# Output halves in f16 parts from batch 0's third column tile on, in pairs of tiles

## The chip, the cores and the metric

The kernel runs on one NeuronCore of a Trainium2 chip. The metric is the device time of one execution in microseconds (us), smaller is better; it is compared as the median of several runs. The engines are TensorE (PE, matrix products; PEld is its weight load), VectorE (DVE), ScalarE (ACT), GpSimd (POOL) and SyncE (SP), which issues the DMAs.

## The reference

Four batches of 12416 tokens with 128 channels pass two attention steps over 32 induced points, and then a SwiGLU layer with 1536 hidden units:

```
def mab(q, kv):
    s = scale * (q @ kv.transpose(0, 2, 1))
    s = s - s.max(-1, keepdims=True)
    a = np.exp(s)
    a /= a.sum(-1, keepdims=True) + 1e-09
    return a @ kv
h = mab(I, x)                  # (4, 32, 128)
x = mab(x, h)                  # (4, 12416, 128), then reshaped to (49664, 128)
g = x @ w_gate                 # (49664, 1536)
silu = g * (1.0 / (1.0 + np.exp(-g)))
val = x @ w_val
out = silu * val @ w_out       # (49664, 128)
```

All of it is in float32.

## The kernel before

The output of the second attention is never written down: `a @ h @ w` is taken as `a @ (h @ w)`, where h has 32 rows. The attention weights of a column tile (up to 512 tokens) are stacked as high and low parts into 128 rows (`st.stack[c]`), and the products of h with the gate and value weights, also in parts, are the stationary operand (`st.w`, or `st.wn` where the parts are float16).

The work runs in slots. Each batch has 25 column tiles (tile 0 holds 4 blocks of each of four token groups, the other 24 hold 15 or 16 blocks of one group), and each column tile has 12 tiles of 128 hidden units, so 300 slots a batch. A slot has these steps:

- `front`: two matmuls, gate and value, into two PSUM banks
- `gate`: silu on ACT; `value`: the product with the value bank on DVE, giving h
- `split`: a rounded copy (hi, on ACT) and the rest (lo, on POOL, for hidden tiles 1, 5 and 9 on DVE)
- `back`: three matmuls into the output accumulator, `w_lo * hi + w_hi * hi + w_hi * lo`; after the twelfth, `evac` copies the accumulator on DVE and a DMA writes it out

In the first column tile of batch 0 (`u.whole`) h and the output weights are not split, and `back` is one float32 matmul, which the profile shows as two records. In column tiles 1 to 12 of batch 0 the parts are in fp32r (float32 words that PE takes in one pass), with the output weights in `wo_hi` and `wo_lo`. From slot 156 on (`CSW = 13`), and in all later batches, the slots run in pairs (`fronts`, `gates`, `values`, `splits`): the parts are float16, a pair's gate and value lie in two double banks of PSUM, and ACT, DVE and POOL take both slots in one instruction. Sometimes (`u.own`) DVE takes over the split of one of the two. For float16 the values must be scaled by powers of two: `peak_of` and `peak_a` to `peak_d` find the largest weights, `size_a` to `size_u` find the scales from h, `half_a` to `half_c` write the scaled output weights in f16 parts into `keep[2]` and `keep[3]`.

PSUM has 8 banks: two (`ps_o`) for the accumulators and some helpers, six for fronts, as six single banks (`ps_gv`) or as three double ones (`ps_two`). `bank()` hands out one of the six to the other steps.

Each engine works its queue in program order, and the program order is written by hand. `START` and `SECOND` list the start as tokens (`f:3` is the front of slot 3, `g` its silu, `m` its product, `k` its back, `P:0:1` a `peak_of`). `FIRST` and `cur.steps` give the other steps of batch 0 and 1 a slot at which they are put into the queues; `plan` gives the steps of the next batch's attention, and `post` those of a column group's attention weights. In each slot (or pair) the loop puts in the front, the silu, the product, the split of the slot before, the steps due, and then as many backs as keep the number of finished but unused tiles at `ahead`:

```
ahead = min(ahead + (1 if b else size) / RAMP, top_) if nxt is not None and slot < last_burst else max(ahead - 1 / RAMP, low_)
if slot in bursts:
    ahead = low_ - (size == 1)
while len(pend) + sum(len(x.us) for x in wait) > ahead + (slot != slots[-1]):
    back(pend.pop(0))
```

`RAMP` is 6; `top_` and `low_` are 9 and 5 for single slots, 14 and 8 for pairs. Bursts are the slots in which ACT does long exponentials: slot 36 and slot 125 in batch 0 (the second is `nxt.e1`), and one more later. Steps that take an accumulator bank (`acc`) wait until no column tile is about to begin or end.

Of the kernel before, what the change touches and what calls it, by code (L numbers as in the profile page):

```python
# [58 lines left out]
DVE_TILES = {1, 5, 9}  # L59
CAST = {11}  # L60
# [22 lines left out]
al:1:0 g:7 X:o2 pk:5 sh:o2 g:8 low:o2 k:4 pm:5 f:9 jn:o2 pc:5 k:5 f:10 sp:1 m:7 k:6 m:8 f:11 g:9 add:o2 k:7 m:9 g:10 g:11 m:10 m:11 hi:o0 lo:o0 hi:o1  # L83
lo:o1
"""
FIRST = {
    12: "sp:2",
    13: "hi:o2",
    14: "lo:o2",
    15: "sp:3",  # L90
# [11 lines left out]
    54: "m2:70:84",
    56: "sb:56:70:1 m2:84:97",
    59: "sb:70:84:1",
    62: "sb:84:97:1",
# [7 lines left out]
def induced_set_attention_then_swiglu(ctx: ExitStack, tc: tile.TileContext, xt, xn, ind, wgv, wo, out):  # L113
# [120 lines left out]
    joint = {}  # L234

    def half_a(i):
        cs = slice(WP * i, WP * i + WP)
        joint[i] = hp.tile([P, 2 * WF], F32, name="h")[:, :WF]
        nc.gpsimd.tensor_add(out=joint[i], in0=wo_hi[:, cs].bitcast(F32), in1=wo_lo[:, cs].bitcast(F32))
# [583 lines left out]
    with tc.tile_pool(name="xt0", bufs=NCH - NXT) as xt0, tc.tile_pool(name="xn0", bufs=NCH - NXN) as xn0:  # L823
# [18 lines left out]
        def run(token):  # L842
# [17 lines left out]
            at=f["aT"], ah=lambda q, e=0: f["a_hi"](q, (f["same"], nc.scalar.copy)[e]),  # L860
# [35 lines left out]
    def value(u):  # L896
        n = u.n
        if u.whole:
            u.h = hip.tile([P, WB], F32, name="h_hi")[:, :WF]
        else:  # L900
            u.h = u.v if u.t in DVE_TILES else hp.tile([P, 2 * WF], F32, name="h")[:, :WF]
# [2 lines left out]
    def split(u):
        if u.whole:
            return
        n = u.n
        u.hi = hip.tile([P, WB], F32R, name="h_hi")[:, u.at[1]:u.at[1] + WF]
        u.lo = lop.tile([P, WB], F32R, name="h_lo")[:, u.at[2]:u.at[2] + WF]
        (nc.vector.tensor_copy if u.cast_dve else nc.scalar.copy)(out=u.hi[:, :n], in_=u.h[:, :n])  # L910
        eng = nc.vector if u.t in DVE_TILES or u.last else nc.gpsimd
        eng.tensor_sub(out=u.lo[:, :n], in0=u.h[:, :n], in1=u.hi[:, :n].bitcast(F32))  # L912
# [5 lines left out]
    def fronts(st, b, c, t):  # L918
        us = []
        g, v = two(), two()  # L920
        for k in range(2):
# [40 lines left out]
    def back(u):  # L962
# [54 lines left out]
    for b in range(B):  # L1017
        nxt = attention(b + 1, (one, oneb)[(b + 1) % 2]) if b + 1 < B else None
        if nxt is not None:
            nxt.steps = plan(nxt, PA if b == 0 else PB, b + 1)  # L1020
            if b == 0:
# [5 lines left out]
                cur.steps += [(14 + 6 * i, lambda i=i: peak_of(0, i)) for i in range(6)]  # L1027
                cur.steps += [(66 + 6 * i, lambda i=i: peak_of(1, i)) for i in range(3)]
                small = [lambda f=f, k=k: f(k) for k in range(2) for f in (peak_a, peak_m, peak_b)] + [peak_c, peak_d]
                sizes = [cur.f["size_" + k] for k in "abcdu"]  # L1030
                small[2].acc = small[5].acc = sizes[1].acc = (NT - 1, 0, 1)
                cur.steps += list(zip((48, 53, 58, 84, 88, 94, 98, 101), small)) + list(zip((62, 68, 78, 82, 108), sizes)) + [(97, cur.f["proj_rounds"])]
# [116 lines left out]
```

## Time and profile before

| | |
|---|---|
| median of 3 runs | 1396.9 us (1396.57 to 1397.24) |
| the profiled execution, first to last instruction (span) | 1394.8 us |
| that execution's own time beside the span | not recorded; the runs' median is 2.1 us above the span |
| PE busy | 1380.5 us (99%) |
| ACT busy | 1219.3 us (87%) |
| POOL busy | 1211.2 us (87%) |
| DVE busy | 1139.9 us (82%) |
| granted PE clock, mean | 0.999 of full speed |

Busy time is the union of the records of an engine. Matmuls are pipelined: a record is longer than the distance to the next one's start, so a busy PE is not yet a PE at its peak. Batch 0's slot 12 begins near 55 us, its slot 156 near 245 us.

### The profile page before, as it was taken

How to read it: one execution, taken by the hardware profiler on the slowest of the kernel's cores; microseconds unless marked ns; L12 is line 12 of the kernel's file. 1: busy time of each engine (PE TensorE's matmuls, PEld its weight loads, DVE VectorE, ACT ScalarE, POOL GpSimd, SP SyncE). 2: the span in 40 equal slices, each digit the busy share in tenths (PEclk: the TensorE clock that was granted, in tenths of full speed). 3: DMA queues.
4: the chain of work that ended last, by engine and by line, in shares of the span. 5: the costliest groups of instructions: out<-in, count | busy, mean ns of one | idle time of the engine just before them, and what ended most of it. 6: DMA issues, size and time to landing. Idle time of an engine off the chain costs nothing.

```text
span 1394.8 us, 21845 instructions
## 1 busy us (share of the span) xinstructions
PE 1380.5 (99%) x7480; PEld 707.9 (51%) x7480; DVE 1139.9 (82%) x1548; ACT 1219.3 (87%) x1481; POOL 1211.2 (87%) x748
## 2 busy tenths in 40 slices
PE   8999999999999999999999999999999999999998
PEld 6577687544444444444444445444444444444444
DVE  6889878878888767888888877878888888888887
ACT  4988798889998898899999888889999989989987
POOL 1679778899999889988999988989999989989987
PEclk9999999999999999999999999999999999999999
DMA  9224523201122432111003423211001010010000
GB/s 374 80 74 152 168 85 123 101 27 53 32 85 91 177 127 76 60 52 30 30 29 121 157 76 131 103 40 48 28 28 33 31 37 25 31 37 31 28 29 29
DMA packets 52335, 107.03 MB, mean 77 GB/s; under 512 B 13440, under 2 KB 34432, under 8 KB 52224
## 3 DMA queue, kind: packets, MB, share of 16 engines
q1 hardware_dynamic: 52224, 105.64, 22.4%
q8 instruction: 59, 0.97, 0.3%
q14 instruction: 52, 0.43, 0.1%
HBM read 62.87 MB, written 25.43 MB: 63 GB/s over the span
## 4 chain that ended last, share of the span: by engine, by line
PE 91%; ACT 6%; DVE 2%; issue 1%; POOL 0%; DVEq 0%; ACTq 0%; POOLq 0%
PE gw L929 30%; PE o L973 17%; PE o L974 17%; PE o L975 17%; PE gv L889 2%; PE gv L888 2%; ACT silu L939 1%; PE o L454 1%; PE gw L369 1%; PE o L369 1%; PE gv L369 1%; ACT silu L894 1%; ACT s_all L633 1%; ACT h_hi L910 1%; PE gv L361 1%
## 5 line engine op out<-in xcount | busy, mean ns | idle before, releaser
L956 POOL TENSOR_TENSOR h_lo<-h,h_hi 128x960 f16<-128x960 f32 (+2 forms) x522 | 977.5, 1894 | 101.1 <-ACT h_hi L954 94.5
L946 DVE SCALAR_TENSOR_TENSOR h<-gw,sc,silu 128x960 f32<-128x960 f32 (+3 forms) x524 | 599.7, 1145 | 191.4 <-ACT silu L939 177.6
L939 ACT ACTIVATE silu<-gw,sc 128x960 f32<-128x960 f32 (+2 forms) x523 | 566.8, 1085 | 119.3 <-PE gw L929 51.4
L954 ACT CAST h_hi<-h 128x960 f16<-128x960 f32 (+3 forms) x517 | 480.5, 930 | 2.8 <-DVE h L946 2.4
L973 PE MATMUL o<-h_hi,work 128*128 128x480 f16 (+1 forms) x1044 | 388.2, 372 | 0.0
L975 PE MATMUL o<-h_lo,work 128*128 128x480 f16 (+1 forms) x1044 | 388.2, 372 | 0.0
L974 PE MATMUL o<-h_hi,work 128*128 128x480 f16 (+1 forms) x1044 | 388.2, 372 | 0.0
L929 PE MATMUL gw<-stack,tw 128*128 128x512 f16 (+1 forms) x1200 | 300.6, 373 | 0.4 <-ACT silu L939 0.4
L929 PE MATMUL gw<-stack,work 128*128 128x480 f16 (+1 forms) x888 | 221.3, 371 | 1.9 <-ACT silu L939 1.5
L929 PEld LDWEIGHTS <-tw 128*128 128x128 f16 x1200 | 117.2, 98 | 135.1 <-issue 2.8
L912 POOL TENSOR_TENSOR h_lo<-h,h_hi 128x512 fp32r<-128x512 f32 x108 | 139.8, 1318 | 33.5 <-ACT h_hi L910 24.2
L973 PEld LDWEIGHTS <-work 128*128 128x128 f16 x1044 | 102.3, 98 | 117.7 <-issue 3.4
L975 PEld LDWEIGHTS <-work 128*128 128x128 f16 x1044 | 102.1, 98 | 115.5
L974 PEld LDWEIGHTS <-work 128*128 128x128 f16 x1044 | 102.1, 98 | 114.5 <-issue 0.5
L929 PEld LDWEIGHTS <-work 128*128 128x128 f16 x888 | 86.3, 98 | 101.1 <-issue 7.2
L894 ACT ACTIVATE silu<-gv 128x512 f32<-128x512 f32 x156 | 93.8, 603 | 15.2 <-PE gv L888 12.2
L902 DVE TENSOR_TENSOR h<-gv,silu 128x512 f32<-128x512 f32 x108 | 73.2, 682 | 18.2 <-ACT silu L894 10.4
L946 DVE SCALAR_TENSOR_TENSOR o<-gw,sc,silu 128x480 f32<-128x480 f32 (+1 forms) x99 | 72.1, 728 | 0.0
L956 DVE TENSOR_TENSOR h_lo<-o,h_hi 128x480 f16<-128x480 f32 (+1 forms) x99 | 66.3, 670 | 3.4
L888 PE MATMUL gv<-stack,tw 128*128 128x512 f32 x156 | 65.4, 419 | 2.7 <-ACT silu L894 1.2
L983 DVE TENSOR_SCALAR ob<-o,sc 128x480 f32<-128x480 f32 (+1 forms) x87 | 62.9, 723 | 3.9 <-PE o L975 3.9
L910 ACT CAST h_hi<-h 128x512 fp32r<-128x512 f32 x95 | 58.9, 620 | 8.1 <-DVE h L902 7.4
(217 smaller groups left out, 1111.6 us busy)
## 6 DMA issues: line engine op xcount, KB each, us to landing
xt_sb<-xt SPq DMA_DIRECT2D x32, 896.0 KB, 5.2
xn_sb<-xn SPq DMA_DIRECT2D x18, 896.0 KB, 5.3
out<-ob SPq DMA_DIRECT2D x52, 256.0 KB, 2.0
out<-ob SPq DMA_DIRECT2D x48, 240.0 KB, 2.0
xt_sb<-xt SPq DMA_DIRECT2D x4, 832.0 KB, 4.5
stack<-a_hi SPq DMA_DIRECT2D x96, 30.0 KB, 1.8
stack<-a_lo SPq DMA_DIRECT2D x96, 30.0 KB, 1.8
xn_sb<-xn SPq DMA_DIRECT2D x3, 832.0 KB, 5.1
```

What stands on the lines that cost most here:

```text
L888: nc.tensor.matmul(out=u.g[:, :n], lhsT=st.w[:, wcol(0, t)], rhs=rhs, start=True, stop=True)
L894: nc.scalar.activation(out=u.s[:, :u.n], in_=u.g[:, :u.n], func=AF.Silu)
L902: nc.vector.tensor_mul(out=u.h[:, :n], in0=u.v[:, :n], in1=u.s[:, :n])
L912: eng.tensor_sub(out=u.lo[:, :n], in0=u.h[:, :n], in1=u.hi[:, :n].bitcast(F32))
L929: nc.tensor.matmul(out=x[:, 512 * (u.t - t):][:, :u.n], lhsT=st.wn[:, wcol(k, u.t)], rhs=st.stack[c][:, :u.n], start=True, stop=True)
L939: nc.scalar.activation(out=f(u.s), in_=f(u.g), func=AF.Silu, scale=u.st.g)
L946: nc.vector.scalar_tensor_tensor(out=h, in0=f(u.v), scalar=u.st.k, in1=f(u.s), op0=ALU.mult, op1=ALU.mult)
L954: (nc.vector.tensor_copy if h is u.x else one_wide if u.cast_dve else nc.scalar.copy)(out=f(u.hi), in_=h)
L956: (nc.vector if h is u.x else nc.gpsimd).tensor_sub(out=f(u.lo), in0=h, in1=f(u.hi))
L973: nc.tensor.matmul(out=o[:, :n], lhsT=w_lo[:, ws], rhs=u.hi[:, :n], start=(t == 0), stop=False)
L974: nc.tensor.matmul(out=o[:, :n], lhsT=w_hi[:, ws], rhs=u.hi[:, :n], start=False, stop=False)
L975: nc.tensor.matmul(out=o[:, :n], lhsT=w_hi[:, ws], rhs=u.lo[:, :n], start=False, stop=(t == NT - 1))
```

## The change

- Column tile 1 of batch 0 (slots 12 to 23) no longer splits: h stays float32, and `back` uses the unsplit pieces of the output weights (`pieces["o0"]` to `["o2"]`), as in column tile 0. The functions `split`, `hi`, `lo`, `half_a` and the tiles `wo_hi` and `wo_lo` are gone.
- From slot 24 on (`CSO = 2`), not from 156, the slots run in pairs with h and the output weights in f16 parts. For column tiles 2 to 12 the fronts still use the fp32r weights `st.w` and the fp32r stack; the silu has scale 1 and the product the new scale `st.kf`.
- The peaks and sizes move from slots 14 to 108 to the end of `SECOND` and slots 12 to 21; `half_b` and `half_c` move from slots 106 to 154 to slots 24 to 34 and read the unsplit pieces. `peak_b` and `size_m` take their bank from `bank()`, no longer from `ps_o`.
- In `FIRST` the scores of batch 0's blocks 70 to 97 move from slot 50 to 56, with what follows them. Batch 1's first scores come in two visits of four and three chunks, as in later batches, no longer chunk by chunk.

```diff
+CSO = 2
 SECOND = """ ...
-... g:10 g:11 m:10 m:11 hi:o0 lo:o0 hi:o1
-lo:o1
+... g:10 g:11 m:10 m:11 sza P:0:0 P:0:1 P:0:2 P:0:3
 FIRST = {
-    12: "sp:2",
-    13: "hi:o2",
-    14: "lo:o2",
-    15: "sp:3",
+    12: "sp:2 P:0:4",
+    13: "P:0:5",
+    14: "Pa:0 Pm:0 P:1:0",
+    15: "sp:3 Pb:0 P:1:1",
+    16: "P:1:2",
+    17: "szb Pa:1",
+    18: "szc Pm:1",
+    19: "Pb:1",
+    20: "Pc",
+    21: "Pd szu",
...
-    50: "s2:52:56:1 s2:56:70 s2:70:84:1 s2:84:97:1",
+    50: "s2:52:56 s2:56:70:1",
...
+    56: "s2:70:84 s2:84:97:1 sb:56:70:1",
...
     def peak_b(k):
-        ps = ps_o.tile([P, 512], F32, name="o")
+        ps = bank()
...
-        nc.scalar.activation(out=keep[2][:, cs], in_=joint[i], func=AF.Copy, scale=top[:, 2:3])
+        nc.scalar.activation(out=keep[2][:, cs], in_=pieces[f"o{i}"].w, func=AF.Copy, scale=top[:, 2:3])
...
         def size_c():
             grow(st.sc[:, 0:2], powers[:, 0:2], st.sc[:, 6:7])
             grow(st.g, powers[:, 2:3], st.low)
+            if b == 0:
+                grow(st.kf, powers[:, 4:5], st.sc[:, 6:7])
+                grow(st.kf, st.kf, st.sc[:, 6:7])
...
-            if b == 1:
-                add(v1 if q < NXT else last, "s1", q, q not in (0, NXT))
-        if b > 1:
-            add(v1, "s1_visit", 0, 1, 2, 3)
-            add(last, "s1_visit", 4, 5, 6)
+        add(v1, "s1_visit", 0, 1, 2, 3)
+        add(last, "s1_visit", 4, 5, 6)
...
     def fronts(st, b, c, t):
+        wn = st.wn if b or c >= CSW else st.w
...
+        u.gs, u.vs = (st.g, st.k) if wn is not st.w or b else (1.0, st.kf)
...
-            nc.scalar.activation(out=f(u.s), in_=f(u.g), func=AF.Silu, scale=u.st.g)
+            nc.scalar.activation(out=f(u.s), in_=f(u.g), func=AF.Silu, scale=u.gs)
...
-            nc.vector.scalar_tensor_tensor(out=h, in0=f(u.v), scalar=u.st.k, in1=f(u.s), op0=ALU.mult, op1=ALU.mult)
+            nc.vector.scalar_tensor_tensor(out=h, in0=f(u.v), scalar=u.vs, in1=f(u.s), op0=ALU.mult, op1=ALU.mult)
...
-            w_hi, w_lo = keep[2:4] if u.half else (wo_hi, wo_lo)
+            w_hi, w_lo = keep[2:4]
...
-                cur.steps += [(106 + 6 * i, lambda i=i: (half_a, half_b, half_c)[i % 3](i // 3)) for i in range(9)]
+                cur.steps += [(24 + 2 * i, lambda i=i: (half_b, half_c)[i % 2](i // 2)) for i in range(6)]
...
-            turn = b == 0 and slot2 == NT * CSW
+            turn = b == 0 and slot2 == NT * CSO
```

## Rows read from the trace of the kernel before

**Rows 1.** The page: the span, and PE's busy time.
```profile
span 1394.8 us, 21845 instructions
...
PE 1380.5 (99%) x7480; PEld 707.9 (51%) x7480; DVE 1139.9 (82%) x1548; ACT 1219.3 (87%) x1481; POOL 1211.2 (87%) x748
```
**Rows 2.** Groups by line of PE, 61.4 to 245.5: count, busy us, mean ns, idle.
```profile
L889 PE MATMUL gv<-stack,tw 128*128 128x512 f32 x140 | 56.3, 402 | 1.5 <-ACT silu L894 1.4
L888 PE MATMUL gv<-stack,tw 128*128 128x512 f32 x139 | 54.6, 393 | 1.2 <-ACT silu L894 1.2
L973 PE MATMUL o<-h_hi,wo_lo 128*128 128x512 f32 x136 | 54.3, 399 | 0.0
...
L454 PE MATMUL o<-xn_sb,eT 128*32 128x128 f32 x194 | 6.1, 274 | 0.2 <-DVE ob L985 0.2
L369 PE MATMUL gv<-xt_sb,hTs 128*32 128x256 f32 (+5 forms) x64 | 4.6, 425 | 0.0
L369 PE MATMUL gv<-xt_sb,indT 128*32 128x448 f32 (+1 forms) x40 | 4.1, 534 | 0.0
L369 PE MATMUL o<-xt_sb,indT 128*32 128x448 f32 x16 | 1.9, 551 | 0.1
L596 PE MATMUL gv<-wgv_sb,hT 128*32 128x384 f32 x16 | 1.5, 492 | 0.0
```
**Rows 3.** Timeline of PE, single slots: start us, us; twelve backs, then a front.
```profile
85.23 0.39 PE L973 MATMUL o<-h_hi,wo_lo 128*128 128x512 f32 x1
...
87.95 0.39 PE L888 MATMUL gv<-stack,tw 128*128 128x512 f32 x1
```
**Rows 4.** Timeline of PE, a pair in batch 1: four fronts, six backs, next pair.
```profile
440.99 1.03 PE L929 MATMUL gw<-stack,tw 128*128 128x512 f16 x4
...
443.14 1.03 PE L929 MATMUL gw<-stack,tw 128*128 128x512 f16 x4
```
**Rows 5.** Timeline of PE, unsplit backs of column 0, one slot apart.
```profile
54.87 1.02 PE L970 MATMUL o<-h_hi,s_all 128*128 128x512 f32 x2
...
56.19 1.02 PE L970 MATMUL o<-h_hi,s_all 128*128 128x512 f32 x2
```
**Rows 6.** Timeline of PE: a mixed cycle after slot 156; then f16 backs alone.
```profile
252.65 0.98 PE L929 MATMUL gw<-stack,work 128*128 128x480 f16 x4
...
254.19 0.98 PE L929 MATMUL gw<-stack,work 128*128 128x480 f16 x4
...
301.52 0.37 PE L973 MATMUL o<-h_hi,work 128*128 128x480 f16 x1
...
304.96 0.37 PE L975 MATMUL o<-h_lo,work 128*128 128x480 f16 x1
```
**Rows 7.** Timeline of PE: three waits, in brackets with what ended them.
```profile
84.20 0.51 PE L889 MATMUL gv<-stack,tw 128*128 128x512 f32 x1 [0.50 <-ACT silu L894]
...
224.09 0.50 PE L888 MATMUL gv<-stack,tw 128*128 128x512 f32 x1 [0.95 <-ACT silu L894]
...
308.85 0.56 PE L929 MATMUL gw<-stack,work 128*128 128x480 f16 x2 [1.09 <-ACT silu L939]
```
**Rows 8.** Timeline of ACT: the burst of slot 36; two silus of pairs.
```profile
86.15 1.28 ACT L633 ACT_TABLE_LOAD   x1
...
89.82 1.09 ACT L894 ACTIVATE silu<-gv 128x512 f32<-128x512 f32 x2
...
424.19 1.11 ACT L939 ACTIVATE silu<-gw,sc 128x1024 f32<-128x1024 f32 x1
...
426.13 1.12 ACT L939 ACTIVATE silu<-gw,sc 128x1024 f32<-128x1024 f32 x1
```
**Rows 9.** Groups by line of ACT, 61.4 to 245.5: half_b and peak_m.
```profile
L243 ACT ACTIVATE work<-h,top 128x512 f16<-128x512 f32 x3 | 2.2, 736 | 0.0
L218 ACT ACTIVATE eT<-ident,peak 128x128 f32<-128x128 f32 x2 | 0.8, 403 | 0.0
```
**Rows 10.** Groups by line of DVE, 61.4 to 245.5: products and peak reductions.
```profile
L902 DVE TENSOR_TENSOR h<-gv,silu 128x512 f32<-128x512 f32 x106 | 71.8, 682 | 16.5 <-ACT silu L894 8.7 <-issue 3.9 <-PE gv L888 1.2
...
L209 DVE TENSOR_REDUCE peak<-wgv_sb 128x1 f32<-128x512 f32 x6 | 4.0, 674 | 0.0
```

More of the change, by code (lines that the diff above doesn't have):

```diff
@@ L58 @@
 GA = 4
-DVE_TILES = {1, 5, 9}
-CAST = {11}
 E0 = 36
@@ L98 @@
     36: "e2:20:52",
-    50: "s2:52:56:1 s2:56:70 s2:70:84:1 s2:84:97:1",
+    50: "s2:52:56 s2:56:70:1",
     51: "m2:52:56",
     52: "sb:52:56:1 m2:56:70",
[L102 to L105, printed above, removed]
+    56: "s2:70:84 s2:84:97:1 sb:56:70:1",
+    58: "m2:70:84",
+    60: "m2:84:97",
+    62: "sb:70:84:1",
+    65: "sb:84:97:1",
 }
@@ L191, in induced_set_attention_then_swiglu @@
     nc.gpsimd.memset(wide, 2.0 ** 127)
-    powers = const.tile([P, 4], F32, name="powers")
-    for i, k in enumerate((TOP, -1 - TOP, -2 * TOP)):
+    powers = const.tile([P, 5], F32, name="powers")
+    for i, k in ((0, TOP), (1, -1 - TOP), (2, -2 * TOP), (4, TOP - 1)):
         nc.gpsimd.memset(powers[:, i:i + 1], 2.0 ** k)
@@ L206, in peak_of @@
     def peak_of(k, i):
-        w = wgv_sb if k == 0 else wo_hi.bitcast(F32)
+        w = wgv_sb[:, WP * i:WP * i + WP] if k == 0 else pieces[f"o{i}"].w
         at = 6 * k + i
-        nc.vector.tensor_reduce(out=peak[:, at:at + 1], in_=w[:, WP * i:WP * i + WP], op=ALU.max, axis=AX.X, apply_absolute_value=True)
+        nc.vector.tensor_reduce(out=peak[:, at:at + 1], in_=w, op=ALU.max, axis=AX.X, apply_absolute_value=True)
     diag = {}
@@ L232, in peak_d @@
         nc.vector.tensor_scalar(out=powers[:, 3:4], in0=top[:, 1:2], scalar1=2.0 ** (1 - 2 * TOP), scalar2=None, op0=ALU.mult)
[L234 to L239, printed above, removed]
     def half_b(i):
         cs = slice(WP * i, WP * i + WP)
-        nc.scalar.activation(out=keep[2][:, cs], in_=joint[i], func=AF.Copy, scale=top[:, 2:3])
+        nc.scalar.activation(out=keep[2][:, cs], in_=pieces[f"o{i}"].w, func=AF.Copy, scale=top[:, 2:3])
     def half_c(i):
         cs = slice(WP * i, WP * i + WP)
-        nc.vector.scalar_tensor_tensor(out=keep[3][:, cs], in0=joint[i], scalar=top[:, 2:3], in1=keep[2][:, cs], op0=ALU.mult, op1=ALU.subtract)
+        nc.vector.scalar_tensor_tensor(out=keep[3][:, cs], in0=pieces[f"o{i}"].w, scalar=top[:, 2:3], in1=keep[2][:, cs], op0=ALU.mult, op1=ALU.subtract)
     def halved(t, n):
@@ L532, in size_m @@
         def size_m(ps=None):
-            st.ssum = ps_o.tile([P, 512], F32, name="o")[:, :66] if ps is None else ps[:, 512 - 66:]
+            st.ssum = bank()[:, :66] if ps is None else ps[:, 512 - 66:]
             nc.tensor.matmul(out=st.ssum[:, 0:M], lhsT=ones, rhs=st.size, start=True, stop=True)
@@ L541, in size_b @@
             c = lambda i, n=1: st.sc[:, i:i + n]
-            st.up, st.k, st.g, st.u, st.low = [c(i) for i in range(5)]
+            st.up, st.k, st.g, st.u, st.low, st.kf = [c(i) for i in range(6)]
             nc.vector.tensor_reduce(out=ps[:, 64:65], in_=ps[:, 0:M], op=ALU.max, axis=AX.X)
@@ L859, in induced_set_attention_then_swiglu @@
             pa=f["proj_a"], pk=f["proj_k"], pb=f["proj_b"], pm=f["proj_m"], pc=f["proj_c"], sM=f["s2_m"], sT=f["s2_t"], sum=f["sum2"], rec=f["rec2"], no=lambda q, e=1: f["norm2"](q, dve_pool[e]),
-            at=f["aT"], ah=lambda q, e=0: f["a_hi"](q, (f["same"], nc.scalar.copy)[e]),
+            P=peak_of, Pa=peak_a, Pm=peak_m, Pb=peak_b, Pc=peak_c, Pd=peak_d, sza=f["size_a"], szb=f["size_b"], szc=f["size_c"], szu=f["size_u"], at=f["aT"], ah=lambda q, e=0: f["a_hi"](q, (f["same"], nc.scalar.copy)[e]),
             al=lambda q, e=1: f["a_lo"](q, dve_pool[e]), sp=f["spread"], **{f"z{i}": f[f"z{i}"] for i in range(9)})
@@ L881, in front @@
         u.b, u.q, u.j, u.t, u.st, u.half = b, q, j, t, st, False
-        u.at = at(c)
         n = u.n = WF if q == 0 else 32 * FC[q]
-        u.whole = b == 0 and c == 0
         rhs = st.stack[c][:, :n]
@@ L897, in value @@
         n = u.n
[L898 to L901, printed above, removed]
+        u.h = hip.tile([P, WB], F32, name="h_hi")[:, :WF]
         nc.vector.tensor_mul(out=u.h[:, :n], in0=u.v[:, :n], in1=u.s[:, :n])
[L904 to L912, printed above, removed]
     def twin(x, u):
@@ L924, in fronts @@
             u.q, u.j = COLS[c]
-            u.b, u.t, u.st, u.whole, u.half = b, t + k, st, False, True
+            u.b, u.t, u.st, u.half = b, t + k, st, True
             u.n = WF if u.q == 0 else 32 * FC[u.q]
@@ L928, in fronts @@
             for u in us:
-                nc.tensor.matmul(out=x[:, 512 * (u.t - t):][:, :u.n], lhsT=st.wn[:, wcol(k, u.t)], rhs=st.stack[c][:, :u.n], start=True, stop=True)
+                nc.tensor.matmul(out=x[:, 512 * (u.t - t):][:, :u.n], lhsT=wn[:, wcol(k, u.t)], rhs=st.stack[c][:, :u.n], start=True, stop=True)
         u.g, u.v, u.us = twin(g, u), twin(v, u), us
+        u.gs, u.vs = (st.g, st.k) if wn is not st.w or b else (1.0, st.kf)
         return u
@@ L967, in back @@
         ws = slice(P * t, P * t + P)
-        if u.whole:
+        if not u.half:
             k = t % (WP // P)
@@ L999, in parts @@
     def parts(u):
-        (splits if u.half else split)(u)
+        if u.half:
+            splits(u)
     pend, wait = [], []
@@ L1026, in induced_set_attention_then_swiglu @@
                     cur.steps += post(cur, q, nc.gpsimd, base)
[L1027 to L1032, printed above, removed]
+                cur.steps += [(82, cur.f["size_d"]), (97, cur.f["proj_rounds"])]
                 for k in range(2 * NG * NG):
                     cur.steps.append((100 + k // 2, lambda k=k: cur.f["proj_spread"](k // (NG * NG), k // NG % NG, k % NG)))
-                cur.steps += [(106 + 6 * i, lambda i=i: (half_a, half_b, half_c)[i % 3](i // 3)) for i in range(9)]
+                cur.steps += [(24 + 2 * i, lambda i=i: (half_b, half_c)[i % 2](i // 2)) for i in range(6)]
                 cur.steps.sort(key=lambda x: x[0])
```

9 lines of the change are left out of this document (1 added, 8 removed).

## The prediction

> **The bound.** I read the page first: TensorE (PE) is busy 1380.5 of 1394.8 us [rows 1], so nearly every microsecond that another engine loses is hidden, and a change is worth what it does to the PE queue: the spacing of matmuls, and the gaps in which PE waits. The profiled execution's span of 1394.8 us lies 2.1 us under the 1396.9 us median of the runs; I make the sum against the span and add the 2.1 us back.
>
> Busy time is not the cost of a matmul, since records overlap: a row of 0.39 us hides a spacing of about 0.23 us. So the second reading is start times in the timeline. In single slots twelve back matmuls in a row, fp32r with 512 columns, start between 85.23 and 87.95: 2.72 / 12 = 0.2267 us each [rows 3]. In pairs of batch 1, ten f16 matmuls of 512 columns take 443.14 - 440.99 = 2.15, so 0.215 us each [rows 4]. An unsplit slot (two fp32r fronts, one true fp32 back that shows as two records) takes 56.19 - 54.87 = 1.32 us [rows 5]; a split one is 5 x 0.2267 = 1.13 us.
>
> The third reading is how much of the stretch that the change touches is waiting. From the first split back to the first paired front, 61.4 to 245.5, are 184.1 us. In it start 140 + 139 fronts and 3 x 136 backs (two of the three back lines are like the first): 687 x 0.2267 = 155.7 us. Attention work takes 6.1 + 4.6 + 4.1 + 1.9 + 1.5 us, and four smaller groups some 1.9 us more: 20.1 us [rows 2]. What is left, 184.1 - 155.7 - 20.1 = 8.3 us, is waiting. The timeline puts it behind ScalarE (ACT): 0.50 us at 84.20 and 0.95 us at 224.09 are waits for a silu [rows 7]. That is all that better overlap can return in this stretch.
>
> **The change.**
>
> Removed and cheaper on PE. Columns 2 to 12 (132 slots) take their three back matmuls in f16 instead of fp32r: 132 x 3 x (0.2267 - 0.215) = 4.6 us less [rows 3, 4]. Their fronts stay fp32r at 0.2267, since for these columns the pair takes st.w and the unhalved stack. The Trainium skill has a rule that speaks against this term: "TensorE: Matmul & The Clock Gate", section "Back-to-back issue gap", gives the gap as columns / 2.4 GHz + 2.5 ns without a word on type, so 215.8 ns for either. The f16 rows agree with it, the fp32r rows don't; by the page this term is nothing and the forecast is about 4.6 us later.
>
> Dearer on PE. Column 1 goes from split to unsplit: 12 x (1.32 - 1.13) = 2.2 us more [rows 3, 5].
>
> Mixing types. From slot 24 to 155 each of 66 pairs goes from f16 backs to fp32r fronts and back again. The nearest rows are the mixed cycles just after today's turn, four f16 fronts of 480 columns and three fp32r backs: 254.19 - 252.65 = 1.54 us. By pure spacings it would be 4 x (304.96 - 301.52) / 17 + 3 x 0.2267 = 1.49 us [rows 3, 6]. So a round trip costs 0.05 us, 66 of them 3.3 us. The lower bound is nothing: ACT runs hard there, and part of the 0.05 may be a late PSUM bank. Twice the row is the upper bound, 6.6 us. I take 2.5 us, near the row.
>
> Other engines' edits. Three hi copies (ACT), three lo subtractions and three rejoining additions (GpSimd), and the splits of column 1, go; none stands before a PE wait in the rows, so I count nothing for them, and the cover is PE's own backlog of finished tiles. Sizes and peaks move from slots 14 to 108 into the end of SECOND and slots 12 to 21. Batch 1's seven score chunks now come in two visits, as batches 2 and 3 do already; the matmuls are the same, so nothing. The unscaled evacuation becomes a scaled one on VectorE (DVE), behind the same wait. No DMA is added; the halves of the output weights are written at slots 24 to 34 from the pieces themselves.
>
> The start, slots 12 to 15. Here is a new chain: peak_b is a matmul on PE that needs peak_m on ACT (0.40 us [rows 9]), that needs peak_a on DVE, that stands behind six reductions of 0.67 us and the products of slots 12, 13 and 14 at 0.68 us [rows 10]: 4.0 + 2.0 + about 0.3 for two small ones + 0.4 = 6.7 us after the last product of column 0. PE reaches peak_b after three unsplit slots and a front pair, 3 x 1.32 + 0.45 = 4.4 us. PE is in order, so everything behind peak_b (the next backs and fronts) waits up to 2.3 us; DVE's starts come closer than its durations, and I take 2.1. The second peak chain, at slots 17 to 19, goes DVE, GpSimd, ACT (four small scalings), PE; I estimate 0.8. Bounds for both: 0 and 5; taken 2.9 us.
>
> Growing the backlog. The loop holds back finished tiles ahead of a burst: in pairs 2/3 of a tile per pair (2/6 per slot) up to 14, against 1/6 per slot up to 9 before. While it grows PE does fewer backs per pair: 4 x 0.2267 + 4/3 x 3 x 0.215 = 1.77 us. ACT's silu and cast of a pair repeat every 426.13 - 424.19 = 1.94 us [rows 8]. So in growth ACT, not PE, sets the pace, by 0.17 us a pair. Slots 24 to 35: ACT has 6 x 1.94 and three half_b of 0.74 [rows 9], 13.9 us; PE has 6 x 0.91, six unsplit backs of 0.87 (1.32 less two fronts) and two split ones of 0.65, 12.0 us: 1.9 us lost. Then growth from 8 to 14 after slot 36 and after slot 125, nine pairs each: 18 x 0.17 = 3.1 at most; score and hacc visits give ACT time meanwhile, so I take 1.8.
>
> Bursts. At slot 36 ACT does an exponential with two table loads, from 86.15 to 89.82 [rows 8], 3.7 us without a silu. A paired burst of today ends in a PE wait of 1.09 us at 308.85 [rows 7]; I take 1.1. The burst at slot 125 has the hacc matmuls beside it: 0.5, between 0 and 2.5.
>
> Sum. PE work: -4.6 + 2.2 + 2.5 = +0.1. Waiting: 2.9 + 1.9 + 1.8 + 1.1 + 0.5 = 8.2 in place of 8.3. Together nothing: span 1394.8, median about 1396.9 us. The turn from single to paired moves from slot 156 to slot 24 and is counted as equal.
>
> **Rivals.** A, faster: the waits go. The paired stretches of today have few of them, the backlog is deeper, and all PE idle time of the whole span is only 14.3 us [rows 1]. Then growth costs nothing, the bursts 1.5, the start 1.5, mixing 1.3: -4.6 + 2.2 + 1.3 + 1.5 + 1.5 - 8.3 = -6.4, median 1390.5. Against it: ACT's work per two slots does not shrink in pairs.
>
> B, slower: ACT is the bound wherever the backlog grows. From slot 24 to 143 a late silu holds the PSUM banks that the next front needs, three double banks where a pair takes two. If growth costs its full 3.1 and 1.9, each burst 2.5, the start 4.0, mixing 3.3: waits 14.0, -4.6 + 2.2 + 3.3 + 14.0 - 8.3 = +6.6, median 1403.5. It decides from waits of 11.1 us on (8.3 + 2.8).
>
> C, slower: f16 backs between fp32r fronts keep 0.2267 us, because the spacing is set by the neighbours' weight loads. In the mixed cycles the f16 fronts keep their own spacing, which speaks against it. It would add 4.6: median 1401.5. The Trainium skill's gap rule, above, has this outcome too.
>
> D, the change does not do what it says: pairs in columns 2 to 12 with fp32r fronts lose to mixing exactly what f16 gains. That is within the forecast.
>
> **The numbers.** A difference under 0.2% (2.8 us) can't be told from none here. My forecast, no change, 0.40; A 0.36; B 0.20; C 0.04. So faster 0.36, same 0.40, slower 0.24. The predicted time is that of no change, 1396.9. The range takes A's centre and most of B: 1390.0 to 1402.5, with 0.1 left out on either side. The likeliest case alone spans 1394 to 1399.5.
>
> **The checks.** Right: backs of columns 2 to 12 spaced 0.215, a pair 2.2 us; column 1's slots 1.32; a PE gap of about 2 us before peak_b near 60 us, and a smaller one some 6 us later; short silu waits on the second fronts of pairs between slots 24 and 54; column 12's evacuation within 3 us of today's. Wrong: no gap at peak_b and PE unbroken to slot 156 would make it A; repeated waits for silu of 0.2 us or more in most pairs up to slot 143 would make it B; f16 spacing of 0.227 makes it C.

## The result: slower by 1.0%

The changed kernel takes 1411.3 us (median of 4 runs, 1409.2 to 1412.8) against 1396.9 us: ratio 1.0101, 95% interval 1.0087 to 1.0116. Forecast was no change, 1396.9 us, with a range up to 1402.5. The profiled execution's span grew from 1394.8 [rows 1] to 1407.4 us. The page of the changed kernel, span and busy time of PE:

```profile
span 1407.4 us, 21357 instructions
...
PE 1381.8 (98%) x7468; PEld 667.2 (47%) x7468; DVE 1128.4 (80%) x1456; ACT 1204.4 (86%) x1348; POOL 1199.1 (85%) x701
```

PE has 1.3 us more work than in [rows 1], in a span that is 12.6 us longer, so nearly all of the loss is PE standing still. To see where, I take one point after the change's stretch in both traces: the evacuation of the fifteenth column on DVE, first in the kernel before, then in the changed one.

```profile
286.67 0.71 DVE L983 TENSOR_SCALAR ob<-o,sc 128x480 f32<-128x480 f32 x1
```
```profile
298.89 0.71 DVE L959 TENSOR_SCALAR ob<-o,sc 128x480 f32<-128x480 f32 x1
```

The difference there, 12.2 us, stays between 12.0 and 12.7 for the 85 columns that follow. So the loss lies before. The waits of PE from 54 us to that point (what PE waited for; us in total, times, longest us), before:

```profile
PE gv L889 <- ACT silu L894: 1.4, 4, 0.5
PE gv L888 <- ACT silu L894: 1.2, 2, 1.0
PE gw L929 <- DVE r L470: 0.4, 1, 0.4
```

and in the changed kernel:

```profile
PE gw L359 <- DVE s_all L611: 5.0, 2, 2.9
PE gw L904 <- ACT silu L915: 3.8, 2, 2.5
PE gv L225 <- ACT eT L221: 3.3, 2, 1.8
PE gw L904 <- DVE h L922: 1.6, 3, 0.7
```

With the groups under 0.4 us, not shown, 3.2 us of waits became 14.2: 11.0 of the 12.2 us. The same shows in the windows view (length, then busy us of PE, PEld, DVE, ACT, POOL with counts, granted clock, DMA share, GB/s), before and after:

```profile
54.00:287.00 233.00, 229.65 (x1266) 161.84 (x1265) 196.78 (x338) 199.12 (x348) 194.12 (x150) 1.00 0.35 113
```
```profile
54.00:299.00 245.00, 230.62 (x1254) 121.24 (x1253) 185.30 (x246) 184.44 (x215) 181.86 (x103) 0.99 0.33 107
```

PE is busy 1.0 us more and idle 11.0 us more (14.4 for 3.35), while DVE, ACT and POOL each lost 11 to 15 us of work, which brought nothing: none of them is the bound over the stretch, only at certain places in it. The places, from PE's timeline (start us, us; in brackets the idle time before and what ended it):

```profile
62.61 0.49 PE L225 MATMUL gv<-eT,ones 128*128 128x128 f32 x2 [1.83 <-ACT eT L221]
...
69.21 0.49 PE L225 MATMUL gv<-eT,ones 128*128 128x128 f32 x2 [1.46 <-ACT eT L221]
...
98.36 0.73 PE L904 MATMUL gw<-stack,tw 128*128 128x512 f32 x2 [1.34 <-ACT silu L915]
...
110.12 0.43 PE L359 MATMUL gw<-xt_sb,hTs 128*32 128x128 f32 x8
113.42 1.72 PE L359 MATMUL gw<-xt_sb,hTs 128*32 128x448 f32 x8 [2.88 <-DVE s_all L611]
...
124.44 0.91 PE L359 MATMUL gw<-xt_sb,hTs 128*32 128x416 f32 x8 [2.14 <-DVE s_all L611]
...
218.99 0.79 PE L904 MATMUL gw<-stack,tw 128*128 128x512 f32 x1 [2.50 <-ACT silu L915]
```

The two matmuls of L225 are peak_b; their waits are the start chain of the forecast. 98.36 and 218.99 are the bursts of slots 36 and 125. The two waits of L359 were not in the forecast. They are batch 0's second scores at slots 50 and 56: score (PE, s2_m), transpose (DVE, s2_t), second score, second transpose, each pair of scores now in the two halves of one double bank of PSUM. The second score waits for the first transpose, which on DVE stands behind a product, a cast and a subtraction of the tile that is being finished (DVE's timeline):

```profile
110.55 1.28 DVE L922 SCALAR_TENSOR_TENSOR h<-gw,sc,silu 128x1024 f32<-128x1024 f32 x1
111.74 0.68 DVE L930 CAST h_hi<-o 128x512 f16<-128x512 f32 x1
112.45 0.69 DVE L932 TENSOR_TENSOR h_lo<-o,h_hi 128x512 f16<-128x512 f32 x1
113.06 0.30 DVE L611 STREAM_TRANSPOSE s_all<-gw 128x128 f32<-128x128 f32 x1
```

In the kernel before, the same order of scores and transposes stood at slot 50, but each of the four scores had a single bank, and PE's timeline has their 32 matmuls in one row without a wait:

```profile
103.51 2.63 PE L369 MATMUL gv<-xt_sb,hTs 128*32 128x128 f32 x32
```

The score at 113.42 takes 1.72 us where the eight matmuls of the same score shape at 121.34 take 0.96: the granted clock has fallen. From 100 to 113 us it was still 1.00. Windows of the changed kernel behind two of the long waits (the granted clock is the number behind POOL's count):

```profile
113.00:117.00 4.00, 3.58 (x14) 1.49 (x15) 1.18 (x4) 0.62 (x1) 1.77 (x2) 0.57 0.71 239
...
219.00:222.00 3.00, 3.00 (x7) 1.74 (x8) 2.94 (x6) 1.90 (x2) 0.53 (x1) 0.50 0.00 0
```

From 113.5 to 116.5 the clock is 0.50, as in the second window. So behind the waits of 2.88 and 2.50 us PE runs for a while at the lower of its two levels, 1.2 GHz, and loses more than it waited. Behind the wait of 2.14 us at 124.44 the clock is 1.00.

What should be cheaper is cheaper. From PE's timeline of the changed kernel, the first and last of 23 backs in a row ahead of a burst, and the fronts of two steady pairs:

```profile
208.66 0.38 PE L950 MATMUL o<-h_hi,work 128*128 128x512 f16 x1
...
213.41 0.38 PE L951 MATMUL o<-h_lo,work 128*128 128x512 f16 x1
```
```profile
145.91 1.28 PE L904 MATMUL gw<-stack,tw 128*128 128x512 f32 x4
...
148.15 0.82 PE L904 MATMUL gw<-stack,tw 128*128 128x512 f32 x2
```

Backs start (213.41 - 208.66) / 22 = 0.2159 us apart, and the pair repeats every 148.15 - 145.91 = 2.24 us. Pure spacings would make 4 x 0.2267 + 6 x 0.2159 = 2.20: mixing costs 0.04 us a pair. Column 1's unsplit backs, where nothing but a slot's fronts stands between them, start 1.32 to 1.33 us apart, as those of column 0 in [rows 5]:

```profile
69.53 1.02 PE L946 MATMUL o<-h_hi,xn_sb 128*128 128x512 f32 x2
...
70.86 1.02 PE L946 MATMUL o<-h_hi,xn_sb 128*128 128x512 f32 x2
```

### The profile page after: what moved, and what is told of

Read it like the earlier page. It is cut to its first block, busy times and chain, and to the rows that moved or that the text cites. A ratio compares the mean times of both kernels' runs of the same rounds, so it can differ in the third digit from the quotient of the medians.

```text
span 1407.4 us, 21357 instructions
## 1 busy us (share of the span) xinstructions
PE 1381.8 (98%) x7468; PEld 667.2 (47%) x7468; DVE 1128.4 (80%) x1456; ACT 1204.4 (86%) x1348; POOL 1199.1 (85%) x701
## 4 chain that ended last, share of the span: by engine, by line
PE 88%; ACT 5%; DVE 3%; DMA 2%; issue 1%; POOL 0%; SPq 0%; DVEq 0%; ACTq 0%; POOLq 0%
PE gw L904 33%; PE o L949 16%; PE o L951 16%; PE o L950 16%; ACT silu L915 2%; PE gw L359 1%; PE o L444 1%; DVE h L922 1%; PE o L359 1%; DMA s_all<-wgv 1%; DMA xt<-xt 1%; ACT s_all L626 1%; PE o L946 1%; ACT h_hi L930 1%; PE gw L589 0%
## 5 line engine op out<-in xcount | busy, mean ns | idle before, releaser
L932 POOL TENSOR_TENSOR h_lo<-h,h_hi 128x1024 f16<-128x1024 f32 (+2 forms) x588 | 1113.0, 1912 | 137.6 <-ACT h_hi L930 128.7
L922 DVE SCALAR_TENSOR_TENSOR h<-gw,sc,silu 128x1024 f32<-128x1024 f32 (+3 forms) x591 | 681.6, 1154 | 227.7 <-ACT silu L915 211.7
L930 ACT CAST h_hi<-h 128x1024 f16<-128x1024 f32 (+3 forms) x581 | 543.7, 936 | 5.6 <-DVE h L922 5.1
L949 PE MATMUL o<-h_hi,work 128*128 128x512 f16 (+1 forms) x1176 | 439.2, 373 | 0.0
L951 PE MATMUL o<-h_lo,work 128*128 128x512 f16 (+1 forms) x1176 | 438.5, 373 | 0.0
L950 PE MATMUL o<-h_hi,work 128*128 128x512 f16 (+1 forms) x1176 | 438.4, 373 | 0.0
L904 PE MATMUL gw<-stack,tw 128*128 128x512 f16 (+2 forms) x1464 | 387.1, 386 | 6.2 <-ACT silu L915 4.2
L915 ACT ACTIVATE silu<-gw 128x1024 f32<-128x1024 f32 x66 | 67.5, 1026 | 38.3 <-PE gw L904 35.3
L959 DVE TENSOR_SCALAR ob<-o,sc 128x512 f32<-128x512 f32 (+1 forms) x98 | 71.1, 725 | 3.9 <-PE o L951 3.9
L930 DVE CAST h_hi<-o 128x480 f16<-128x480 f32 (+1 forms) x106 | 70.1, 661 | 0.1
L904 PEld LDWEIGHTS gw<-stack,tw 128*128 128x128 f32 x264 | 49.8, 194 | 28.8 <-ACT silu L915 5.6
```

Of the source, the lines that this page charges most:

```text
L904: nc.tensor.matmul(out=x[:, 512 * (u.t - t):][:, :u.n], lhsT=wn[:, wcol(k, u.t)], rhs=st.stack[c][:, :u.n], start=True, stop=True)
L922: nc.vector.scalar_tensor_tensor(out=h, in0=f(u.v), scalar=u.vs, in1=f(u.s), op0=ALU.mult, op1=ALU.mult)
L930: (nc.vector.tensor_copy if h is u.x else one_wide if u.cast_dve else nc.scalar.copy)(out=f(u.hi), in_=h)
L932: (nc.vector if h is u.x else nc.gpsimd).tensor_sub(out=f(u.lo), in0=h, in1=f(u.hi))
L949: nc.tensor.matmul(out=o[:, :n], lhsT=w_lo[:, ws], rhs=u.hi[:, :n], start=(t == 0), stop=False)
L950: nc.tensor.matmul(out=o[:, :n], lhsT=w_hi[:, ws], rhs=u.hi[:, :n], start=False, stop=False)
```

## The experiments

Each ratio is to the kernel before on the same chip, with its 95% interval; times are medians of 4 to 11 runs, with 1397.0 to 1397.2 us for the kernel before.

**1. The order of the second scores alone.** Both scores of a slot first, then both transposes:

```
-    50: "s2:52:56 s2:56:70:1",
+    50: "sM:52:56 sM:56:70:1 sT:52:56 sT:56:70",
-    56: "s2:70:84 s2:84:97:1 sb:56:70:1",
+    56: "sM:70:84 sM:84:97:1 sT:70:84 sT:84:97 sb:56:70:1",
```

> The changed kernel, but at slots 50 and 56 both score matmul groups are queued before both transposes, so the second half of the double bank is written before the first is read. Theory 1 (the second group waits for the first's transpose only because both lie in one double bank): the two TensorE waits of 2.9 and 2.1 us go, no half-speed clock stretch follows near 113 us, and the time falls by 5 to 7 us against the changed kernel. Theory 2 (VectorE is simply late here): the wait moves to the next front and the time stays within 1.5 us.

Measured: 1403.3 us (1401.8 to 1404.2), ratio 1.0044 (1.0030 to 1.0058): 8.0 us faster than the changed kernel. PE's timeline has the sixteen matmuls of both scores in one row, with no wait ahead of it, and the clock stays up:

```profile
110.11 1.18 PE L359 MATMUL gw<-xt_sb,hTs 128*32 128x128 f32 x16
```
```profile
113.00:117.00 4.00, 3.95 (x18) 2.05 (x16) 4.00 (x8) 3.16 (x5) 4.00 (x4) 1.00 0.70 235
```

This is more than the 5.0 us of waits. The profiled executions differ by 7.4 us (1407.4 and 1400.0), and two stretches hold nearly all of it. From column 2's evacuation (107.98 in both) to column 4's (144.94 and 138.69) it is 6.25: the 5.0 of waits and 1.2 beside them. From column 9's to column 10's:

```profile
221.01 0.74 DVE L959 TENSOR_SCALAR ob<-o,sc 128x512 f32<-128x512 f32 x1
242.30 0.74 DVE L959 TENSOR_SCALAR ob<-o,sc 128x512 f32<-128x512 f32 x1
```
```profile
214.77 0.74 DVE L959 TENSOR_SCALAR ob<-o,sc 128x512 f32<-128x512 f32 x1
235.13 0.74 DVE L959 TENSOR_SCALAR ob<-o,sc 128x512 f32<-128x512 f32 x1
```

The first two rows are the changed kernel's, the last two this one's: 21.29 us against 20.36. Both have the same wait of 2.50 us there; the changed kernel's clock falls behind it and this one's does not. So one fall costs about 0.9 us here, and about 1.2 at slot 50.

**2. The peak chains later.** The first peak_b moves from slot 15 to 17, the second peak_m from 18 to 17, so that its peak_b at 19 has two slots, and the sizes come a slot or two later:

```
-    15: "sp:3 Pb:0 P:1:1",
+    15: "sp:3 P:1:1",
...
-    17: "szb Pa:1",
-    18: "szc Pm:1",
+    17: "Pb:0 Pa:1 Pm:1",
+    18: "szb",
...
-    20: "Pc",
+    20: "szc Pc",
```

> The changed kernel, but peak_b runs at slots 17 and 19 instead of 15 and 19, with peak_m of the second before the scalings and the scalings at slot 20. Theory 1 (TensorE waits in order for the peak chain): the waits of 1.8 and 1.5 us go and the time falls by 3 to 4 us. Theory 2 (the lost time is VectorE's load at the start): other waits of the same size appear before slot 24 and the time stays within 1 us.

Measured: 1407.9 us (1407.2 to 1410.2), ratio 1.0077 (1.0065 to 1.0090), 3.4 us faster than the changed kernel. The waits before L225 shrink from 3.3 to 0.2 us, and a new one of 0.7 us appears on a front, behind a product on DVE. Moving the chain returns about its forecast size.

**3. Both.** The edits of 1 and 2 together; the base of the experiments from 5 on.

> Both edits of the two kernels above. If they are separate causes, the time falls by the sum, 8 to 11 us against the changed kernel, which leaves some 2 to 6 us over the kernel before. If one shadows the other, by less than 7 us.

Measured: 1400.8 us (1399.6 to 1402.9), ratio 1.0025 (1.0015 to 1.0034): 10.5 us faster than the changed kernel, where the parts add up to 11.4. The two causes hardly overlap and carry nearly three quarters of the 14.5 us. Of the 7.0 us of waits left in the changed stretch (54 to 291 us), the two largest groups:

```profile
PE gw L904 <- ACT silu L915: 3.8, 2, 2.5
PE gw L904 <- DVE h L922: 1.6, 3, 0.7
```

These are the two bursts and the waits in the growth of the backlog. The rest is 1.6 us in five groups, the new 0.7 of experiment 2 among them.

**4. Column 1 unsplit, alone, in the kernel before.**

```
-        u.whole = b == 0 and c == 0
+        u.whole = b == 0 and c <= 1
```

> The kernel before with one part of the change alone: column tile 1 of batch 0 unsplit, with one true float32 back per slot. Theory (the back's TensorE time alone counts): 12 x 0.187 = 2.2 us slower than before. Rival (the splits that fall away free ScalarE, and that returns it): no change, within 1 us.

Measured: 1398.6 us (1398.1 to 1399.6), ratio 1.0010 (1.0001 to 1.0019): 1.4 us slower. In its trace the columns from 5 on stand 1.4 us later than in the kernel before, so the cost is there. The slots by themselves give 2.2, so 0.8 comes back, and the trace shows most of it: PE waits for silus for 2.0 us from 54 to 288 us, where the kernel before waits 2.6.

**5. ACT's three half_b earlier** (on 3: half_b at slots 22, 22 and 23 instead of 24, 28 and 32, half_c at 24, 26 and 28).

> The kernel with scores reordered and peaks later, and the three scalings of the output weights to f16 on ScalarE moved from slots 24, 28, 32 to slots 22, 22, 23, where ScalarE has no casts. Theory 1 (they make ScalarE late while the backlog grows after slot 24): the TensorE waits of 0.3 and 0.7 us near 84 to 89 us go and the time falls by 1 to 1.5 us. Theory 2 (ScalarE sets the pace there by its silu and cast alone): within 0.5 us.

Measured: 1400.9 us (1400.0 to 1402.3), ratio 1.0027 (1.0017 to 1.0037), the same as 3. Half_b's place does not matter: the growth after slot 24 does not lose its time to them. What the waits there end on is a product on DVE, and the changed kernel's DVE timeline shows it behind half_c (L243) and an evacuation (the last line is PE's):

```profile
87.82 1.25 DVE L243 SCALAR_TENSOR_TENSOR work<-s_all,top,work 128x512 f16<-128x512 f32 x1
...
89.59 1.27 DVE L922 SCALAR_TENSOR_TENSOR h<-gw,sc,silu 128x1024 f32<-128x1024 f32 x1
```
```profile
90.91 1.20 PE L904 MATMUL gw<-stack,tw 128*128 128x512 f32 x4 [0.70 <-DVE h L922]
```

The wait of 0.28 us at 86.76 follows another half_c, of 2.47 us. This run moves half_c by two to six slots as well, but keeps it in the growth; the wait of 0.28 is gone there, that of 0.7 is not. No run takes half_c out of the growth.

**6. The burst of slot 125 without batch 0's second exponential** (on 3; it leaves that exponential out).

```
-                cur.steps.append((nxt.e1, lambda: run(f"e2:52:{NTB}")))
+                pass
```

> The same base kernel; it leaves out batch 0's exponential of blocks 52 to 97 at the burst of slot 125 (some 1.4 us of ScalarE there), so those attention weights stay logits. Theory 1 (the wait of 2.5 us at that burst is ScalarE's block of some 7.7 us outlasting the backlog): the wait shrinks to about 1.2 us, no half-speed stretch follows it, and the time falls by 2.5 to 3.5 us. Theory 2 (something else ends that wait): the time stays within 0.5 us.

Measured: 1399.8 us (1398.6 to 1400.6), ratio 1.0018 (1.0010 to 1.0027), 0.9 us faster, which the two intervals do not separate from none. In PE's timeline the wait at the burst is halved:

```profile
209.67 0.73 PE L904 MATMUL gw<-stack,tw 128*128 128x512 f32 x2 [1.21 <-ACT silu L915]
```

The clock stays at 1.00 behind it. The cause is the right one: in the profiled executions this run is 2.1 us further ahead of 3 behind the burst (column 11) than ahead of it. Then it loses 1.9 us in batches 1 and 2, where PE waits 1.1 us for two loads of xn_sb that 3 does not wait for; whether that follows from the edit or is chance is open. ACT's timeline of the changed kernel at this burst shows what the backlog has to cover:

```profile
210.20 1.28 ACT L626 ACT_TABLE_LOAD   x1
211.50 1.41 ACT L626 ACTIVATE s_all<-s_all 128x1440 f32<-128x1440 f32 x1
...
216.62 1.28 ACT L915 ACT_TABLE_LOAD   x1
217.92 1.94 ACT L915 ACTIVATE silu<-gw 128x1024 f32<-128x1024 f32 x2
```

From 210.20 to 217.92 ACT makes no silu: 7.7 us, twice the 3.7 of slot 36's burst [rows 8], and the exponential left out is 1.41 of it. The kernel before has the same 7.7 us there (200.47 to 208.19) without a wait for a silu. PE's timelines show a difference besides the pairs, first before, then after:

```profile
206.44 2.60 PE L454 MATMUL o<-xn_sb,eT 128*32 128x128 f32 x84 [0.16 <-DVE ob L985]
```
```profile
225.34 2.60 PE L444 MATMUL o<-xn_sb,eT 128*32 128x128 f32 x84
```

These are batch 1's hacc matmuls. Before, PE did them while ACT made no silu; in the changed kernel they come only behind the wait at 218.99. No run moved them, so their share in the 2.50 us is not shown.

**7. Fronts of columns 2 to 12 in f16** (on 3). They read a constant f16 tile, so that only their time means something:

```
-  lhsT=wn[:, wcol(k, u.t)], rhs=st.stack[c][:, :u.n]
+  lhsT=wn[:, wcol(k, u.t)] if wn.dtype == F16 else flat[:, 0:P], rhs=st.stack[c][:, :u.n] if wn.dtype == F16 else flat[:, :u.n]
```

> The same base kernel, with the fronts of columns 2 to 12 of batch 0 reading a constant f16 tile in place of the fp32r weights and stack, so their outputs are meaningless. Theory 1 (mixing types and the fp32r spacing cost TensorE time in each pair): 66 x (4 x 0.0107 + 0.03) = 4 to 5.5 us less. Theory 2 (ScalarE sets the pace there): less than 2 us.

Measured: 1395.9 us (1394.9 to 1397.6), ratio 0.9993 (0.9984 to 1.0002), 4.9 us faster than 3. The sum says 66 pairs x 0.04 = 2.6 for mixing and 264 x (0.2267 - 0.2159) = 2.9 for the spacing, 5.5 together; the run agrees. So the two together are real time at the end, and nearly as large as the spacings say; the run does not tell one from the other.

**8. Three more edits at once** (on 5): the peak reductions spread over slots 8 to 11, a backlog of up to 16 tiles in the pairs of batch 0, and the burst of slot 125 leaving 6 of them.

> The same base kernel with the scalings early, the first peak reductions spread between the products of slots 8 to 11, and in batch 0's pairs a backlog of up to 16 tiles, of which the burst of slot 125 leaves 6. Theory (each remaining wait has a cause of its own and no other takes its place): 4 to 6 us under the base kernel, so 0.5 to 2.5 us under the kernel before. Rival (the waits move on, since ScalarE has no time to give): within 2 us of the base kernel.

Measured: 1404.9 us (1402.0 to 1405.5), ratio 1.0051 (1.0038 to 1.0064), 4 us slower. The long wait at slot 125 is gone. PE's timeline has a new one of 1.17 us for a silu at 118.38, while the larger backlog grows, and one behind the burst, at the next step that needs what the backlog had covered:

```profile
249.28 0.49 PE L512 MATMUL o<-fold,hn 128*128 128x128 f32 x2 [3.47 <-DVE hn L467]
```

This is batch 1's h_c: PE reaches it before DVE has finished the norm ahead of it. In experiment 11, with 8 tiles kept behind the burst instead of 6 and the larger backlog only from slot 62 on, neither wait appears.

**9. The waits of slots 50 and 56 filled** with 18 and 14 small matmuls of no use, in the changed kernel itself, so that PE does not stand still there:

```
-    50: "s2:52:56 s2:56:70:1",
+    50: "sM:52:56 wq:52:18 sT:52:56 s2:56:70:1",
-    56: "s2:70:84 s2:84:97:1 sb:56:70:1",
+    56: "sM:70:84 wq:70:14 sT:70:84 s2:84:97:1 sb:56:70:1",
...
+        def warm2(b0, n):
+            for i in range(n):
+                nc.tensor.matmul(out=cur.sp[b0][:, 448:512], lhsT=ones, rhs=ident[:, 0:64], start=True, stop=True)
```

> The changed kernel, with 18 and 14 small extra matmuls (64 columns, into unused columns of the first score bank) queued between the two score groups at slots 50 and 56, so that TensorE works through most of each wait for VectorE's transpose; the waits themselves stay. Theory 1 (the idle gap lets the granted clock fall to half, and that costs time of its own): no half-speed stretch near 113 and 124 us, and 1.5 to 3 us less than the changed kernel. Theory 2 (only the waits cost): within 1 us of the changed kernel.

Measured: 1411.5 us (1410.7 to 1412.3), ratio 1.0104 (1.0090 to 1.0118): no change. The trace shows that this test was not clean. PE's timeline:

```profile
110.94 0.43 PE L359 MATMUL gw<-xt_sb,hTs 128*32 128x128 f32 x8
111.29 4.23 PE L834 MATMUL gw<-ident,ones 128*128 128x64 f32 x36
115.93 0.96 PE L359 MATMUL gw<-xt_sb,hTs 128*32 128x448 f32 x8 [0.41 <-DVE s_all L611]
...
123.32 3.34 PE L834 MATMUL gw<-ident,ones 128*128 128x64 f32 x28
127.41 0.91 PE L359 MATMUL gw<-xt_sb,hTs 128*32 128x416 f32 x8 [0.74 <-DVE s_all L611]
```

The score after the filling takes 0.96 us instead of 1.72: the clock did not fall. But the second scores come 1.7 and 1.9 us later behind the first than in the changed kernel, since the filling lasts longer than the wait was, and there is still a wait for the transpose after it. From column 2's evacuation to column 4's (108.80 to 147.90) it is 39.10 us, 2.1 more than the 36.96 of the changed kernel, not 3.6 more. So some 1.4 us seem to have come back with the clock, in accord with the 1.2 of experiment 1, and the filling took them and more.

**10. A slower growth of the backlog** (on 3: 1/6 of a tile per slot in batch 0's pairs, as in the single slots of the kernel before, instead of 2/6).

> The kernel with scores reordered and peaks later, with the backlog of batch 0's pairs growing at 1/6 of a tile per slot in place of 2/6. Theory 1 (in fast growth ScalarE sets the pace): the waits of 0.3 to 0.7 us between 84 and 108 us shrink and the time falls by 1 to 2 us. Theory 2 (the backlog is worth more than its growth costs): the bursts of slots 36 and 125 wait longer and the time is the same or up to 2 us more.

Measured: 1403.2 us (1402.2 to 1405.3), ratio 1.0046 (1.0034 to 1.0059), 2.4 us slower than 3. The burst of slot 36 now ends in

```profile
98.09 0.73 PE L904 MATMUL gw<-stack,tw 128*128 128x512 f32 x2 [2.32 <-ACT silu L915]
```

instead of 1.34, and another wait grows to 1.7 us. A smaller backlog at the burst costs more than quick growth does.

**11. The best of these** (on 5: the peak reductions spread as in 8, and the backlog up to 16 tiles only between slots 62 and 125, back to 8 behind the burst).

```
-            top_, low_ = ((HI, SKEW), (HI2, SKEW2))[size - 1]
+            top_, low_ = ((HI, SKEW), (HI2 + 2 * (b == 0 and 62 <= slot2 < nxt.e1 + 1), SKEW2))[size - 1]
```

> Scores reordered, peaks later, scalings early, the first peak reductions spread between the products of slots 8 to 11, and the backlog of batch 0's pairs up to 16 tiles between slots 62 and 125, back to 8 at the burst. Theory (the wait of 2.5 us at the burst is a backlog two to four tiles too small): that wait halves, no half-speed stretch follows, and the time is 2 to 3 us under the 1400.8 us of the base kernel. Rival (more backlog only moves the wait to its growth): within 1 us.

Measured: 1398.4 us (1397.8 to 1400.1), ratio 1.0011 (1.0002 to 1.0020). 13.0 of the 14.5 us are won back, and 1.3 us are left to the kernel before. The forecast of this run holds: the wait at the burst is 1.20 us and the clock stays at 1.00 behind it. In its trace PE waits for 5.1 us from 54 to 288 us, 3.1 of them for silus, against 3.2 before. No version that was run and computes the output beats the kernel before.

## Why the prediction was wrong, step by step

**Right.** The f16 backs have the forecast spacing, 0.2159 us, so by the spacings 4.3 to 4.6 us came off PE's work; rival C is out. Column 1's slots cost 1.32 us. Mixing costs 0.04 us a pair, 2.6 in all, for 2.5. The start chain stands where it was put, with waits of 1.83 and 1.46 us for 2.1 and 0.8; moving it away returned 3.4 us for the forecast 2.9. The burst of slot 36 waits 1.34 us for 1.1.

**Smaller than forecast, and by another mechanism.** At the turn and in growth there are waits of 0.3 to 0.7 us, 1.9 in all (0.3 at the turn), for 3.7. They end on DVE's products of h, not on silus as the check expected, half_b has no part in them, and half_c on DVE, which the forecast did not count, stands ahead of two of them (experiment 5). The check on column 12 failed too: its evacuation came 11.3 us later (270.70 for 259.40), not within 3.

**The first step that failed** is the costing of the score visits: "score and hacc visits give ACT time meanwhile". The visits of batch 1 were costed at nothing, and the regrouping of batch 0's second scores at slots 50 and 56, which the diff shows, was not costed at all. With single banks two scores were independent. In pairs they share a double bank, and in the order written by hand a transpose on DVE came between them. That is 5.0 us of PE waits, and putting both scores ahead of both transposes gave back 8.0 us with the clock, which did not fall at either place there. The halves do not overlap, so the wait seems to belong to the double bank as a whole; this is inferred from the wait, its disappearance in experiment 1, and the same order in single banks without a wait, not tried by itself.

**Mis-sized.** The burst of slot 125 was taken at 0.5 us, with bounds 0 to 2.5; it waits 2.50, because ACT is without a silu for 7.7 us there and the backlog of 14 does not reach. The kernel before showed these 7.7 us already. The second exponential is 1.41 us of them, and without it the wait was 1.21 (experiment 6). The hacc matmuls, which the forecast put beside the burst, came 6 us behind the wait's end.

**The second step that failed**, and as large, is the term for the old waits: "What is left, 184.1 - 155.7 - 20.1 = 8.3 us, is waiting". The windows view of the kernel before gives PE's busy time in the same stretch:

```profile
61.40:245.50 184.10, 180.80 (x1027) 136.74 (x1026) 158.12 (x282) 156.79 (x292) 152.25 (x123) 1.00 0.37 121
```

PE is idle for 3.3 us there, and the last column of [rows 2] says nearly the same: 1.5 + 1.2 + 0.2. The other 5.0 us are what counts and spacings left over while PE is busy; what they are stays open. So "8.2 in place of 8.3" gave back 5.1 us that were no waits: with 3.2 the forecast's own sum is +5.1 us, 1402.0 us. Against these 3.2 us stand 14.2 us of waits after.

**Missing.** That the clock could fall was in no term. It cost the profiled execution some 2.1 us (1.2 + 0.9). The runs of the changed kernel with the mean granted clock at 0.997, 0.996, 0.994 and 0.995 took 1409.2, 1410.5, 1412.2 and 1412.8 us.

**The rivals.** The waits passed the 11.1 us from which B decides, and B's side won, but not by B's mechanism: the largest term waits for DVE behind a shared bank. That B's 14.0 us of waits meet the measured 14.2 is luck, since it has no scores in it and 5.0 us for growth; its time, 1403.5, is too low mostly by the same 8.3 (with 3.2 its sum is +11.7). ACT ends the waits of the two bursts alone (and of the start chain, by peak_m, at the end of a chain that DVE makes late). A fails where it said that the start and bursts cost 3.0: they cost 7.1.

In short: start 3.3, score order 5.0, bursts 3.8, turn and growth 1.9, the last 0.2, less 3.2 of old waits, make 11.0 of the 12.2 us. The remaining 1.2 is the change of PE's busy time, to which the clock adds and the f16 backs subtract; I did not split it further. Against the forecast's terms the 12.2 us are 5.1 of old waits that were none, 5.0 for the scores, 2.2 more for the bursts, 0.4 more for the start, 1.8 less for growth, 0.2 for the last wait and 1.1 more PE work. 2 us more lie between the profiled execution (the fastest of the four runs) and the median.

## What to carry to other kernels

When tiles are joined into pairs, list every hand-placed step that takes a bank in the paired stretch, and see which two of them now share one: here a read between two writes of such a pair made the second write wait until the reader's queue had come to it (2.88 and 2.14 us). Put a group's matmuls ahead of all its readers. Take the idle time of a stretch from the profile, not as what is left over from counts and spacings (3.3 us, not 8.3). Cost a burst by the time for which the other engine delivers nothing (3.7 us at one, 7.7 at the other) against what the backlog holds, and when a wait goes, look where the next step is that the backlog had covered (experiment 8: one wait went, 3.47 us came).

## What was not expected of the hardware

A PE wait can cost more than its length, when the granted clock falls behind it. In the profile of the changed kernel the clock went to the 1.2 GHz level behind the waits of 2.88 and 2.50 us, and about 1.2 and 0.9 us more were lost; behind 2.14 us and less it stayed at 1.00. The length of the wait alone does not settle it. Behind the same 2.50 us at slot 125 the clock fell in the profiles of experiments 2, 3 and 10 and stayed at 1.00 in those of 1, 5 and 9; it fell behind 2.13 us in experiment 2 (0.59 over the next 3 us) and stayed at 1.00 behind 3.47 us in experiment 8. What decides it is open.

Changing between f16 backs and fp32r fronts costs 0.04 us per pair, small but, with fp32r's 0.2267 us spacing for f16's 0.2159, 4.9 us in 66 pairs (experiment 7). The Trainium skill ("TensorE: Matmul & The Clock Gate", section "Back-to-back issue gap") gives the gap of a matmul by itself as columns / 2.4 GHz + 2.5 ns, without a word on type; that makes an estimate of 215.8 ns at 512 columns. The f16 rows here agree (0.2159 us), the fp32r rows of the kernel before do not (0.2267 us, [rows 3]).
